# Order of slot 0's weight splits, its gates' gathers and the first weight conversions in a fused attention and two-MLP kernel

## The chip, the cores and the metric

One core of one Trainium2 chip runs the whole program. The metric is the time of one execution on the device, in microseconds (us). A core has TensorE (PE: matmuls; PEld: its weight loads), VectorE (DVE), ScalarE (ACT), GpSimd (POOL) and SyncE (SP). Each engine takes its own instructions strictly in order and waits on semaphores for the others. DMAs are issued by SyncE and, where the rows are picked by an index list, by GpSimd.

## The reference, cut to what matters

```python
x = attention(q, k, v)        # windowed and block-summary attention, 2 x 768 tokens, 8 heads of 64
idx = argmax(normalised(x) @ normalised(expert_emb).T / tau)     # one of 8 experts for a token
out[mask_e] = gate[mask_e] * (relu(x[mask_e] @ w1[e]) @ w2[e])    # 512 -> 1024 -> 512, for each expert e
h = out @ w_in                                                    # 512 -> 2048
g = (a0 + a1*h + a2*h*h + a3*h**3) / (1 + |b0|*|h| + |b1|*h*h + 1e-6)
return g @ w_out                                                  # 2048 -> 512
```

The precision wanted is that of float32, so a product is computed as three: high half by high half, low half by high half, high half by low half. A "split" makes the halves of one block of 128 x 1024 weights: ScalarE copies the block rounded into `whi` (`shi`), and `slo` subtracts that from the block to give `wlo`.

## The kernel before, in words

**Stages.** Attention and the router run first, up to about 102 us. The tokens are then sorted by expert into slots of 128 rows (17 in this run), and the slots are worked off one by one up to about 316 us. The dense second MLP follows, up to the end.

**A slot.** `gather(s)` (GpSimd, indirect DMA) fetches the slot's 128 rows from `xs` in DRAM into one of three buffers `xg`. `xtr(s)` transposes them on TensorE; ScalarE makes the high half (`xhi`, for slot 1 the upper part of `hhi`), VectorE the low half. `gemm1(s)` multiplies by w1 in 24 matmuls of 512 columns. For the first three slots it runs eight with the high half of x, then eight with its low half (the low pass), then eight with `wlo`. `relu(s)` is on ScalarE. `htr(s)` transposes the hidden rows in two halves (ScalarE high, VectorE low). `gemm2(s)` multiplies by w2 in 24 matmuls, and `gemm2e(s)` scales by the gate in `gts` on ScalarE. The program issues `gemm1(s)` before `gemm2(s - 1)`, so TensorE works on two slots in turn.

**Weights.** `wload(s, part)` has SyncE load four blocks of 512 KB of w1 (part 0) or w2 (part 1). From slot 2 on, a load is made only where a flag in the table `rg` says that the expert changes. `wsplit(s, part)` does the splits of four blocks under the same flag, for which ScalarE and VectorE each load the flag of `rg` into a register (lines 896 and 904, `values_load`) and branch. Slots 0 and 1 always have the weights of experts 0 and 1, but `wsplit(1, 0)` reads its flag all the same. Slot 0's splits are not conditional: `l0` to `l3` in the list below are the low splits of its w1 blocks, `slo(0, 4 + k)` those of its w2 blocks.

**The table.** `table()` is a chain of 16 small steps on VectorE, each `tb` in the list being one. The last (lines 758 to 773, called the tail here) writes all of `rg`: each slot's expert, the row of its results, and the flags. The list of row indices for the gathers does not need the tail.

**The written-out order.** `DRAIN` (lines 65 to 68) is the order by hand of the work between attention and the slots: `g0`, `g1` are gather(0) and gather(1), `x0` is xtr(0), `z0`, `z1`, `rc`, `rg` are the gates' softmax (`rg` here is `router_g`, lines 527 to 531, not the table), `F5` gives the indices of slots 1 and on, `k2b` is two matmuls that only keep TensorE busy. `SE` names the engine of `l0` to `l3`, D for VectorE and P for GpSimd. After it the program continues with lines 1161 to 1249.

**Gates.** A slot's gate is column 512 of its row in `xs`, stored by `gw` (SyncE) once `router_g` is done. Slots 0 and 1 are gathered before that, so `regather` fetches their rows once more, and `gate0` copies the column into `gts`, on GpSimd. From slot 2 on, VectorE copies it in `xtr` (line 685).

**Conversions.** The second MLP's weights are stored as 64-bit words. While the slots run, jobs of 128 x 512 words (two a slot) turn them into float32: `conv_load` (SyncE), `conv_a` (ScalarE), `conv_c` (a clamp, GpSimd, line 926), `conv_b` in three steps (VectorE, lines 931 to 937), `conv_s` (store).

Of the kernel before, what the change touches and what calls it, by code (L numbers as in the profile page):

```python
# [58 lines left out]
STOP = False  # L59
MICRO = True  # L60
TRACE = []
SE = "DDDD"
NX, NM = 22, 26
TS, OS = (), (0, 2)
DRAIN = ("E4 T2 h3 E4 S E4 w8 w9 O3 M O2 T1 Z8 O1 d3 X m8 E3 E3 m8 E3 f9 E2 E2 E2 T0 f10 Z9 E1 u3 p3 p3 p3 u3 u3 R0 "
# [3 lines left out]
NEG = 1.0e30  # L69
RS = 1536  # L70
NA = E * RS // P
# [10 lines left out]
def tile_kernel(ctx, tc, I, out):  # L82
    nc = tc.nc
# [457 lines left out]
    def wload(s, part, ks=range(4)):  # L541
        r = rw[s % 2, part]
        src = I["w1"] if part == 0 else I["w2"]
        if s > 1:
            ev = nc.sync.value_load(rg[0:1, 1, s:s + 1], min_val=0, max_val=E - 1)
            fl = nc.sync.value_load(rg[0:1, 3, s:s + 1], min_val=0, max_val=1)
        for k in ks:
            if s < 2:
                nc.sync.dma_start(out=r[:, k], in_=src[s, :, k])
            else:  # L550
                nc.sync.dma_start(out=r[:, k],
                                  in_=src[bass.ds(ev, 1), :, k].rearrange("o p f -> (o p) f"), cond=fl > 0)
# [95 lines left out]
    def gather(s):  # L648
        xg[s] = gx[s % 3]
        nc.gpsimd.indirect_dma_start(out=xg[s], out_offset=None, in_=xs,  # L650
                                     in_offset=bass.IndirectOffsetOnAxis(ap=idx[:, s:s + 1], axis=0))
# [38 lines left out]
    def slo(s, i, eng):  # L690
        eng.tensor_tensor(out=wlo[:, i], in0=rw[s % 2, i // 4][:, i % 4], in1=whi[:, i].bitcast(F32), op=ALU.subtract)  # L691
# [232 lines left out]
    def conv_c(j, eng):  # L924
        z = cvt[j][1].bitcast(F32)
        eng.tensor_scalar(out=z, in0=z, scalar1=CLO, scalar2=CHI, op0=ALU.max, op1=ALU.min)  # L926
# [23 lines left out]
    hsb = {}  # L950

    def gemm1(s, between=None):
        hi, lo = xTm.pop(s)
        if s == 1:
            ph = [ps_g.tile([P, 4, P], F32, name="hg").rearrange("p a b -> p (a b)") for n in range(2)]
        else:
            ph = [ps_h.tile([P, 512], F32, name=f"ph{n}") for n in range(2)]
        for rl in (False, True):
            ls = (hi,) if rl else (hi, lo)
            knl = [(k, n, l) for k in range(4) for n in range(2) for l in ls]  # L960
            if s < 3:
                knl.sort(key=lambda x: x[2] is lo)
            for k, n, l in knl:
                if between and l is lo and (k, n) == (2, 0):
                    between()
                w = (wlo if rl else whi)[:, k, 512 * n:512 * n + 512]
                nc.tensor.matmul(out=ph[n], lhsT=l[:, k], rhs=w, start=(k == 0 and not rl and l is hi),  # L967
                                 stop=(k == 3 and rl))
        hsb[s] = (hb, ph)
# [4 lines left out]
            nc.scalar.activation(out=h[:, 4 * n:4 * n + 4], in_=ph[n].rearrange("p (a b) -> p a b", a=4),  # L974
                                 func=AF.Relu)

    def htr(s):
        h, _ = hsb.pop(s)
        hi, lo = hhl
        for n in range(2):  # L980
            pt = ps_ht.tile([P, 4, P], F32, name=f"pht{n}")
            for k in range(4):
                nc.tensor.transpose(out=pt[:, k], in_=h[:, 4 * n + k], identity=ident)
            c = slice(4 * n, 4 * n + 4)
            nc.scalar.activation(out=hi[:, c], in_=pt, func=AF.Copy)  # L985
            nc.vector.tensor_tensor(out=lo[:, c], in0=pt, in1=hi[:, c].bitcast(F32), op=ALU.subtract)  # L986
        hTm[s] = (hi, lo)
# [159 lines left out]
    def regather(s):  # L1147
        nc.gpsimd.indirect_dma_start(out=xg[s], out_offset=None, in_=xs,
                                     in_offset=bass.IndirectOffsetOnAxis(ap=idx[:, s:s + 1], axis=0))

    def gate0(s):
        regather(s)
        nc.gpsimd.tensor_copy(out=gts[:, s:s + 1], in_=xg.pop(s)[:, DM:DM + 1])

    NSL = MAXS - 2
# [6 lines left out]
        conv_load(j)  # L1162
    gw()
    gather(2)
    gate0(0)
    gather(3)
    gemm1(0, lambda: xtr(1))
    gate0(1)
    wload(2, 0)
    wload(1, 1)  # L1170
    for j in job_at[2]:
        conv_load(j)
    wsplit(1, 0)
    relu(0)
    for k in range(2, 4):
        shi(0, 4 + k)
    for k in range(2):
        slo(0, 4 + k, nc.vector)
    for s in range(1, NSL + 1):
        mine = job_at.get(s, ())  # L1180
        if s == NX // 2 + 1:
            cx_.close()
            xb = ctx.enter_context(tc.tile_pool(name="xb", bufs=1, reuse_waits="tile"))
            x2.append((xb.tile([P, 4, TT], F32R, name="x2h0"), xb.tile([P, 4, TT], F32R, name="x2l0")))
        if 1 < s < NSL - 2:
            gather(s + 2)
        if s > 1:
            ysave(s - 2)
        if s >= NSL - 2:
            fsplit(s - (NSL - 2), 0)  # L1190
        if s >= NSL - 3:
            fload(s - (NSL - 3), 0)
        if s < NSL:
            gemm1(s)
            if STOP and s == 1:
                cx_.close()
                moe.close()
                rawr.close()
                return
            if s == 1:  # L1200
                htr(0)
                for k in range(2, 4):
                    slo(0, 4 + k, nc.vector)
                wload(2, 1)
            if s + 2 < NSL:
                wload(s + 2, 0)
            if s >= NSL - 6:
                x2load(s - (NSL - 6))
            for j in job_at.get(s - 1, ()):
                conv_s(j)  # L1210
            for j in job_at.get(s + 1, ()):
                if s > 1:
                    conv_load(j)
            if 1 < s < NSL - 1:
                wload(s + 1, 1)
            if s + 1 < NSL:
                wsplit(s + 1, 0, "h")
            relu(s)
            if s + 1 < NSL:
                if s != 1:  # L1220
                    xtr(s + 1)
                wsplit(s + 1, 0, "l")
            for j in mine:
                conv_a(j)
            for j in mine:
                conv_c(j, nc.gpsimd)
        if s > 0:
            gemm2(s - 1)
            if s == 1:
                xtr(2)  # L1230
            if s == NSL - 1:
                wsplit(s, 1, "h")
                htr(s)
            if s == NSL:
                elem_a(0)
                fsplit(3, 0, nc.gpsimd)
                elem_b(0)
            gemm2e(s - 1)
            if s == NSL - 1:
                wsplit(s, 1, "l")  # L1240
                fg1(0)
            if 0 <= s - (NSL - 5) < 4:
                x2prep(s - (NSL - 5))()
        if s < NSL - 1:
            htr(s)
            wsplit(s, 1)
        for j in mine:
            for k in range(3):
                conv_b(j, k)
    fload(0, 1)  # L1250
# [289 lines left out]
```

## Time and profile before

| what | value |
|---|---|
| three runs | 597.63, 600.44, 600.63 us; median 600.44 |
| the profiled execution | 601.18 us, of which the span is 599.4 |
| busy: PE, DVE, ACT, POOL | 572.9 (96%), 475.9 (79%), 418.1 (70%), 265.6 us (44%) |
| mean granted TensorE clock | 0.987 of full speed |
| chain that ended last | it can be followed back to 327.19 us; almost all of it is PE: matmuls of line 1335 20% of the span, 946 to 948 5%, 5% and 4% |

The busy share is a mean over stages. The chain of waits, followed back from the last instruction, runs through TensorE's matmuls alone until the last 27 us, and it says nothing of the slots, since TensorE has no pause there from which it could step to another engine. For these one reads the stretches (how long TensorE is idle in each), then its waits, and then each engine's time line, where the bracket behind a row gives the idle time before an instruction and what ended it. A row's start minus the start of the row before it on the same engine is what an instruction costs its engine; its duration is a little longer, as neighbours overlap.

### The profile page before, as it was taken

How to read it: one execution, taken by the hardware profiler on the slowest of the kernel's cores; microseconds unless marked ns; L12 is line 12 of the kernel's file. 1: busy time of each engine (PE TensorE's matmuls, PEld its weight loads, DVE VectorE, ACT ScalarE, POOL GpSimd, SP SyncE). 2: the span in 40 equal slices, each digit the busy share in tenths (PEclk: the TensorE clock that was granted, in tenths of full speed). 3: DMA queues.
4: the chain of work that ended last, by engine and by line, in shares of the span. 5: the costliest groups of instructions: out<-in, count | busy, mean ns of one | idle time of the engine just before them, and what ended most of it. 6: DMA issues, size and time to landing. Idle time of an engine off the chain costs nothing. (4 is left out here: it accounts for less than half of the span.)

```text
span 599.4 us, 10320 instructions
## 1 busy us (share of the span) xinstructions
PE 572.9 (96%) x3149; PEld 467.7 (78%) x3149; DVE 475.9 (79%) x1032; ACT 418.1 (70%) x722; POOL 265.6 (44%) x281
## 2 busy tenths in 40 slices
PE   4879998999999999999999999999999999999995
PEld 3768985787888888888887888888888888888884
DVE  6999988969755797588767888988988777777885
ACT  6969845673625755467766998777778887767673
POOL 6476161157443461634132564523535664432334
PEclk9889997999999999999999999999999999999999
DMA  9988934577678997798983434020244300100101
GB/s 299 324 252 283 341 117 122 173 252 249 239 234 296 346 322 232 249 323 305 374 261 93 132 96 125 27 79 1 61 133 140 89 1 1 52 19 0 54 17 71
DMA packets 38750, 101.66 MB, mean 170 GB/s; under 512 B 6105, under 2 KB 6233, under 8 KB 38690
## 3 DMA queue, kind: packets, MB, share of 16 engines
q1 hardware_dynamic: 36210, 92.81, 46.4%
q0 software_dynamic: 2480, 8.15, 4.3%
q8 instruction: 26, 0.43, 0.3%
q14 instruction: 34, 0.28, 0.1%
HBM read 119.51 MB, written 19.18 MB: 231 GB/s over the span
## 5 line engine op out<-in xcount | busy, mean ns | idle before, releaser
L926 POOL TENSOR_SCALAR el<-el 128x512 f32<-128x512 f32 x32 | 66.5, 2088 | 92.5 <-ACT el L921 92.5
L691 DVE TENSOR_TENSOR wlo<-rw,whi 128x1024 fp32r<-128x1024 f32 x64 | 77.1, 1262 | 1.3 <-ACT whi L688 0.9
L1135 POOL TENSOR_TENSOR wlo<-el,whi 128x512 fp32r<-128x512 f32 (+1 forms) x32 | 40.9, 1278 | 73.2 <-ACT whi L1133 35.6
L688 ACT ACTIVATE whi<-rw 128x1024 fp32r<-128x1024 f32 x64 | 62.7, 1051 | 6.0 <-DVEq L905 3.9
L998 PE MATMUL py<-whi,hhi 128*128 128x512 f32 x136 | 53.8, 404 | 0.2 <-ACT hhi L985 0.2
L998 PE MATMUL py<-whi,hlo 128*128 128x512 f32 x136 | 52.7, 396 | 0.0
L967 PE MATMUL ph<-whi,xlo 128*128 128x512 f32 x128 | 48.8, 398 | 1.3 <-DVE gts L685 1.3
L967 PE MATMUL ph<-whi,xhi 128*128 128x512 f32 x128 | 49.8, 407 | 0.3 <-ACT xhi L681 0.3
L986 DVE TENSOR_TENSOR hlo<-pht,hhi 128x512 fp32r<-128x512 f32 x34 | 21.8, 681 | 28.9 <-ACT y L1005 16.2
L1119 ACT ACTIVATE el<-el 128x512 f32<-128x512 f32 (+1 forms) x50 | 30.8, 615 | 14.3 <-DVE el L1113 14.3
L946 PE MATMUL hg<-x2h,whi 128*128 128x512 f32 (+1 forms) x100 | 39.0, 390 | 0.0
L1335 PE MATMUL acc<-whi 128*128 128x512 f32 x128 | 38.8, 393 | 0.0
L947 PE MATMUL hg<-x2h,wlo 128*128 128x512 f32 (+1 forms) x100 | 38.7, 387 | 0.0
L948 PE MATMUL hg<-x2l,whi 128*128 128x512 f32 (+1 forms) x100 | 38.6, 386 | 0.0
L1335 PE MATMUL acc<-whi,wlo 128*128 128x512 f32 x128 | 38.5, 391 | 0.0
L1135 POOL TENSOR_TENSOR xlo<-el,xhi 128x512 fp32r<-128x512 f32 (+1 forms) x17 | 20.9, 1230 | 39.5 <-issue 21.0
L1335 PE MATMUL acc<-wlo,whi 128*128 128x512 f32 x128 | 38.4, 390 | 0.0
L1111 ACT ACTIVATE el<-hg,ab 128x512 f32<-128x512 f32 (+1 forms) x33 | 22.2, 674 | 23.0 <-PE hg L948 23.0
L1005 ACT ACTIVATE y<-py,gts 128x512 f32<-128x512 f32 x17 | 11.7, 686 | 36.9 <-PE py L998 36.8
L1120 ACT ACTIVATE el<-el,ab 128x512 f32<-128x512 f32 (+1 forms) x50 | 35.4, 708 | 1.6
L1113 DVE SCALAR_TENSOR_TENSOR el<-el,ab,hg 128x512 f32<-128x512 f32 (+1 forms) x33 | 24.1, 730 | 14.9 <-ACT el L1112 14.6
L1125 DVE SCALAR_TENSOR_TENSOR el<-el,ab,hg 128x512 f32<-128x512 f32 (+1 forms) x33 | 24.1, 729 | 14.6 <-ACT hg L1121 13.9
(600 smaller groups left out, 1654.5 us busy)
## 6 DMA issues: line engine op xcount, KB each, us to landing
rw<-w SPq DMA_DIRECT2D x136, 512.0 KB
cx<-wio SPq DMA_DIRECT2D x22, 512.0 KB
wf<-el SPq DMA_DIRECT2D x32, 256.0 KB
vw<-vp SPq DMA_DIRECT2D x16, 292.5 KB
ys<-y SPq DMA_DIRECT2D x17, 257.0 KB
xg<-wf SPq DMA_DIRECT2D x13, 256.0 KB
xs<-xall SPq DMA_DIRECT2D x12, 257.0 KB
x<-ys SPq DMA_DIRECT2D x12, 257.0 KB
```

The costliest lines, as they stand in the source:

```text
L688: nc.scalar.activation(out=whi[:, i], in_=rw[s % 2, i // 4][:, i % 4], func=AF.Copy)
L691: eng.tensor_tensor(out=wlo[:, i], in0=rw[s % 2, i // 4][:, i % 4], in1=whi[:, i].bitcast(F32), op=ALU.subtract)
L926: eng.tensor_scalar(out=z, in0=z, scalar1=CLO, scalar2=CHI, op0=ALU.max, op1=ALU.min)
L946: nc.tensor.matmul(out=o, lhsT=lh, rhs=rh, start=start, stop=False)
L947: nc.tensor.matmul(out=o, lhsT=ll, rhs=rh, start=False, stop=False)
L948: nc.tensor.matmul(out=o, lhsT=lh, rhs=rl, start=False, stop=stop)
L967: nc.tensor.matmul(out=ph[n], lhsT=l[:, k], rhs=w, start=(k == 0 and not rl and l is hi), stop=(k == 3 and rl))
L998: nc.tensor.matmul(out=py, lhsT=l[:, f], rhs=w, start=(f == 0 and not rl and l is hi), stop=(f == 7 and rl))
L1119: nc.scalar.activation(out=a, in_=a, func=AF.Abs)
L1120: nc.scalar.activation(out=r, in_=a, func=AF.Ln, bias=ab[:, 7:8])
L1135: eng.tensor_tensor(out=lo, in0=g, in1=hi.bitcast(F32), op=ALU.subtract)
L1335: nc.tensor.matmul(out=acc[q], lhsT=l[:, q * P - o:(q + 1) * P - o], rhs=r, start=start, stop=stop)
```

## The change

It has six parts:

- In `DRAIN` the low split `l0` goes ahead of `x0`, `l1` ahead of `z0`, `l2` ahead of `rg` (`router_g`), and the last `tb`, the table's tail, goes from ahead of `x0` to the end of the list.
- `l3` goes to GpSimd (`SE`), and so do the low splits of slot 0's w2 blocks 2 and 3 (blocks 6 and 7 of eight), which stood behind `htr(0)` on VectorE and now stand with the first two.
- `htr(0)` is cut in two: its first half is issued inside `gemm1(1)`, before the fifth matmul of the low pass, and its second half behind that product, with both `conv_a` between them on ScalarE.
- The first conversion's clamp goes to VectorE, and its `conv_b` goes from behind slot 1's w2 splits to ahead of `gemm2(0)`'s part of the program.
- On GpSimd `regather(0)` stays where it was, but `gate0(0)`, gather(3) and `regather(1)` go from around `gemm1(0)` to behind the first clamp, and `gate0(1)` behind `gemm2e(0)`.
- On SyncE `wload(1, 1)` goes ahead of `wload(2, 0)`.

```diff
@@ -59,13 +59,13 @@
 STOP = False
 MICRO = True
 TRACE = []
-SE = "DDDD"
+SE = "DDDP"
 NX, NM = 22, 26
 TS, OS = (), (0, 2)
 DRAIN = ("E4 T2 h3 E4 S E4 w8 w9 O3 M O2 T1 Z8 O1 d3 X m8 E3 E3 m8 E3 f9 E2 E2 E2 T0 f10 Z9 E1 u3 p3 p3 p3 u3 u3 R0 "
          "E1 m9 E1 p3 O0 m9 Z10 R1 E0 E0 h4 d4 E0 w10 w11 u4 m10 f11 p4 Z11 p4 m10 q10 q9 p4 C p4 q11 n0 n1 u4 m11 u4 n2 n2 "
          "i0 m11 h5 d5 n2 p5 PC k2a tb p5 n2 tb p5 n2 p5 F1 tb F2 g0 i2 tb n2 tb F3 k4b i1 tb tb tb tb tb i3 tb K0 k3a tb tb "
-         "K1 k1a tb K2 k1b tb j0 j1 F4 F5 g1 tb x0 k2b z0 z1 rc l0 rg l1 l2 l3 ")
+         "K1 k1a tb K2 k1b tb j0 j1 F4 F5 g1 l0 x0 k2b l1 z0 z1 rc l2 rg l3 tb ")
 NEG = 1.0e30
 RS = 1536
 NA = E * RS // P
@@ -974,10 +974,10 @@
             nc.scalar.activation(out=h[:, 4 * n:4 * n + 4], in_=ph[n].rearrange("p (a b) -> p a b", a=4),
                                  func=AF.Relu)
 
-    def htr(s):
-        h, _ = hsb.pop(s)
+    def htr(s, ns=(0, 1)):
+        h, _ = hsb[s]
         hi, lo = hhl
-        for n in range(2):
+        for n in ns:
             pt = ps_ht.tile([P, 4, P], F32, name=f"pht{n}")
             for k in range(4):
                 nc.tensor.transpose(out=pt[:, k], in_=h[:, 4 * n + k], identity=ident)
@@ -1149,7 +1149,6 @@
                                      in_offset=bass.IndirectOffsetOnAxis(ap=idx[:, s:s + 1], axis=0))
 
     def gate0(s):
-        regather(s)
         nc.gpsimd.tensor_copy(out=gts[:, s:s + 1], in_=xg.pop(s)[:, DM:DM + 1])
 
     NSL = MAXS - 2
@@ -1162,20 +1161,18 @@
         conv_load(j)
     gw()
     gather(2)
-    gate0(0)
-    gather(3)
+    regather(0)
     gemm1(0, lambda: xtr(1))
-    gate0(1)
+    wload(1, 1)
     wload(2, 0)
-    wload(1, 1)
     for j in job_at[2]:
         conv_load(j)
     wsplit(1, 0)
     relu(0)
     for k in range(2, 4):
         shi(0, 4 + k)
-    for k in range(2):
-        slo(0, 4 + k, nc.vector)
+    for k in range(4):
+        slo(0, 4 + k, nc.vector if k < 2 else nc.gpsimd)
     for s in range(1, NSL + 1):
         mine = job_at.get(s, ())
         if s == NX // 2 + 1:
@@ -1191,16 +1188,16 @@
         if s >= NSL - 3:
             fload(s - (NSL - 3), 0)
         if s < NSL:
-            gemm1(s)
+            gemm1(s, (lambda: htr(0, (0,))) if s == 1 else None)
             if STOP and s == 1:
                 cx_.close()
                 moe.close()
                 rawr.close()
                 return
             if s == 1:
-                htr(0)
-                for k in range(2, 4):
-                    slo(0, 4 + k, nc.vector)
+                for j in mine:
+                    conv_a(j)
+                htr(0, (1,))
                 wload(2, 1)
             if s + 2 < NSL:
                 wload(s + 2, 0)
@@ -1220,10 +1217,16 @@
                 if s != 1:
                     xtr(s + 1)
                 wsplit(s + 1, 0, "l")
-            for j in mine:
+            for j in mine if s > 1 else ():
                 conv_a(j)
             for j in mine:
-                conv_c(j, nc.gpsimd)
+                conv_c(j, nc.vector if j == 0 else nc.gpsimd)
+            if s == 1:
+                for k in range(3):
+                    conv_b(0, k)
+                gate0(0)
+                gather(3)
+                regather(1)
         if s > 0:
             gemm2(s - 1)
             if s == 1:
@@ -1236,6 +1239,8 @@
                 fsplit(3, 0, nc.gpsimd)
                 elem_b(0)
             gemm2e(s - 1)
+            if s == 1:
+                gate0(1)
             if s == NSL - 1:
                 wsplit(s, 1, "l")
                 fg1(0)
@@ -1244,7 +1249,7 @@
         if s < NSL - 1:
             htr(s)
             wsplit(s, 1)
-        for j in mine:
+        for j in mine if s > 1 else mine[1:]:
             for k in range(3):
                 conv_b(j, k)
     fload(0, 1)
```

## Rows read from the trace of the kernel before

**Rows 1.** stretches; columns: stretch, us, busy us of each engine (instructions), granted clock, DMA share, GB/s.

```profile
37.20:40.60 3.40, 0.44 (x2) 0.20 (x2) 3.33 (x8) 0.76 (x2) 3.24 (x4) 1.00 0.83 207
40.60:44.00 3.40, 3.29 (x16) 2.96 (x18) 2.96 (x20) 1.24 (x4) 3.09 (x5) 0.50 0.32 120
91.80:98.60 6.80, 6.80 (x46) 4.10 (x46) 5.04 (x38) 2.93 (x9) 0.60 (x1) 0.50 0.55 159
144.80:573.00 428.20, 427.89 (x1952) 347.95 (x1951) 332.96 (x483) 301.89 (x475) 185.17 (x155) 1.00 0.46 155
```

**Rows 2.** waits of TensorE, 95 to 330 us; columns: us, times, longest.

```profile
PE ph L967 <- DVE wlo L691: 0.4, 1, 0.4
...
PE py L998 <- ACT hhi L985: 0.2, 1, 0.2
```

**Rows 3.** time line of TensorE; columns: start, us, instruction, count [idle before it].

```profile
110.34 2.13 PE L967 MATMUL hg<-whi,hhi 128*128 128x512 f32 x8
112.31 2.03 PE L967 MATMUL hg<-whi,hlo 128*128 128x512 f32 x8
...
138.68 0.51 PE L967 MATMUL ph<-whi,xlo 128*128 128x512 f32 x1 [1.32 <-DVE gts L685]
...
142.30 2.34 PE L967 MATMUL ph<-wlo,xhi 128*128 128x512 f32 x8
```

**Rows 4.** time line of VectorE, behind slot 1's splits.

```profile
133.26 0.83 DVE L931 TENSOR_SCALAR el<-el 128x512 int32<-128x512 int32 x1 [1.82 <-POOL el L926]
```

**Rows 5.** time line of VectorE, 101.7 to 111 us.

```profile
101.84 0.51 DVE L758 TENSOR_TENSOR pr<-ge,dv 128x342 f32<-128x342 f32 x1
...
103.36 0.68 DVE L682 TENSOR_TENSOR xlo<-pht,xhi 128x512 fp32r<-128x512 f32 x1
103.96 0.24 DVE L482 TENSOR_TENSOR zs<-zs,m 128x96 f32<-128x96 f32 x1
...
104.52 1.22 DVE L691 TENSOR_TENSOR wlo<-rw,whi 128x1024 fp32r<-128x1024 f32 x1
105.66 0.24 DVE L529 TENSOR_REDUCE rw__710<-zs 128x12 f32<-128x96 f32 x1
...
106.29 3.43 DVE L691 TENSOR_TENSOR wlo<-rw,whi 128x1024 fp32r<-128x1024 f32 x3
```

**Rows 6.** time line of ScalarE, 102.5 to 118.5 us.

```profile
106.82 0.60 ACT L681 ACTIVATE hhi<-px__1802 128x512 fp32r<-128x512 f32 x1 [1.94 <-PE px__1802 L679]
107.78 3.91 ACT L688 ACTIVATE whi<-rw 128x1024 fp32r<-128x1024 f32 x4 [0.36 <-DVE wlo L691]
```

**Rows 7.** line 904, 100 to 130 us; columns: ns min/median/max, first and last start.

```profile
L904 ACTq TENSOR_LOAD <-rg x2: 273/387/501, 106.8 to 124.6; - x2
```

**Rows 8.** groups of GpSimd, 316 to 590 us; columns: busy us, mean ns | idle before.

```profile
L1135 POOL TENSOR_TENSOR wlo<-el,whi 128x512 fp32r<-128x512 f32 x31 | 40.1, 1295 | 70.6 <-issue 34.8 <-ACT whi L1133 33.0 <-DMA xg<-xs,idx 1.0
```

**Rows 9.** time line of GpSimd in the attention stage.

```profile
36.55 2.06 POOL L196 TENSOR_TENSOR kw<-qk,one 128x1128 f32<-128x1128 f32 x1
```

**Rows 10.** time line of GpSimd, 98 to 147 us.

```profile
102.19 0.99 POOL L650 DMA_INDIRECT xg<-xs,idx  x1 [2.98 <-DVE idx L809]
...
129.34 1.01 POOL L1153 COPY gts<-xg 128x1 f32<-128x1 f32 x1 [5.92 <-DMA xg<-xs,idx]
130.33 4.79 POOL L926 TENSOR_SCALAR el<-el 128x512 f32<-128x512 f32 x2
```

**Rows 11.** time line of VectorE in the attention stage.

```profile
36.12 2.66 DVE L190 COPY el<-ks 128x288 f32<-128x288 f32 x1
```

**Rows 12.** lines 190 and 448, all of the run; columns as in rows 7.

```profile
L190 DVE COPY kw<-ks x6: 311/314/770, 4.8 to 53.4; 128x288 f32<-128x288 f32 x6
...
L448 DVE TENSOR_TENSOR oh<-cst,i x6: 145/176/583, 53.6 to 93.5; 128x16 bf16<-128x16 f32 x6
```

**Rows 13.** instructions and gathers on tile xg, 97 to 147 us.

```profile
L679 PE MATMUL px__2176<-cst,xg x4: 272/272/273, 130.1 to 130.4; 128*128 128x128 f32 x4
...
DMA to landing us min/median/max: 3.4/4.5/8.3
```

## The prediction

> **What bounds the kernel now.** I read the stretches first, then what TensorE waited for, then the time lines of the engines around slot 0. From 144.8 us to 573 us TensorE is busy for 427.89 of 428.20 us [rows 1]: whatever time it has at 144.8 us reaches the end unchanged, and no later stall is there to swallow a gain or a loss. The change touches only the stretch from 102 to 145 us, so the question is when TensorE gets to slot 2's second product, at 144.8 us in this trace. Before that its waits are few: 0.4 us for slot 0's low weights, 0.2 us for slot 0's hidden rows [rows 2], and the largest, 1.32 us for the low half of slot 3's rows [rows 3]. The cause of the last is readable: VectorE stood 1.82 us for GpSimd's clamp of the first conversion [rows 4], so xlo came late and TensorE resumed at 138.68 us. With the slower pace around these waits all this is some 3 us, 0.5% of the run, and that is about what a measurement can tell from no change: the change cannot win much more.
>
> **Part 1: slot 0's splits ahead of the table's tail.** The tail (the last `tb`) writes the table `rg`. VectorE now runs it from 101.84 us to xlo's start at 103.36, 1.52 us [rows 5]. Behind it stand xlo (0.60 us to the next start), z0 and z1 (0.56), a split (1.14), the gates' sums (0.63) and three more splits [rows 5]. In the new order VectorE does split 0, xlo, split 1, z0, z1, split 2, the sums, and only then the tail; split 3 goes to GpSimd. Split 0 fits in front of xlo, which needs ScalarE's high half first; I leave its start at 103.36. So 103.96 + 1.14 + 0.56 + 1.14 + 0.63 = 107.4 us for the tail's start and 109.0 for its end. The splits themselves come in time, which takes away TensorE's 0.4 us wait for them and the slower pace around it: the first product ends near 109.2 us instead of 110.3, where slot 1's begins now [rows 3].
>
> Who waits for the tail? `wsplit(1, 0)` is conditional: ScalarE loads a flag of `rg` into a register (line 904) before it may make slot 1's four high weight blocks. In this trace the flag is over 3 us old by then and costs only its load. The load is issued behind hhi at 106.82 and the first block starts at 107.78, 0.95 us later [rows 6]; the load itself takes 0.27 to 0.50 us [rows 7], so 0.72 to 0.95 us lie between flag and block, and I take 0.85, between the two. In the changed kernel ScalarE stands at that load until the table exists: 109.0 + 0.85 = 109.8 us instead of 107.78. Queued behind it on ScalarE are the four blocks, relu(0), slot 0's high blocks 6 and 7 and the high halves of the hidden rows, and TensorE waits for each of these. The one wait removed is replaced by a longer one.
>
> **Part 2: split 3 on GpSimd beside VectorE's split 1.** No row shows a 128x1024 subtraction on GpSimd. Twice the 128x512 one is 2.59 us [rows 8], and a product with 1128 columns took 2.06 [rows 9]; I take 2.4, nearer to the same operation. It starts when gather(1) has been issued, 102.19 + 0.99 = 103.2 us [rows 10], and ends about 105.6, before TensorE wants it. The price is on VectorE. A copy of 0.31 us [rows 12] took 2.66 when it met a GpSimd product from 36.55 to 38.61: it ended 0.17 us after that one [rows 9, 11]. That copy reads one SBUF tensor; an operation that reads two (L448) took 583 ns once against 145 to 176 [rows 12]. So split 1, which wants to start at 103.96, is held until shortly before GpSimd is done, 105.5 us: +1.6. The ends are nothing, if splits are not held, and the whole 2.4, if the order falls badly. With 1.6 the table is ready at 110.6 and ScalarE's first block starts at 111.4 us, 3.6 later than now. The Trainium skill (SBUF — State Buffer, section "SBUF: two separate sides") says that VectorE and GpSimd share a port pair under an exclusive lock held for a whole instruction, and names VectorE operations with two SBUF inputs among those that it stops. The rows agree as far as they go, and by that page a split that is not held, rival A below, would be ruled out.
>
> The consequence on TensorE: the four blocks take 3.91 us [rows 6], so the last is ready at 115.3; two matmuls later, at 115.8 us, the low pass of slot 1 begins. Now it begins at 112.31 [rows 3]. **+3.5 us.**
>
> **Part 3: slot 0's hidden rows transposed inside slot 1's product.** The eight transposes are the same; with four of them earlier, gemm2(0) need not wait for the first half. That saves the 0.2 us wait [rows 2] and about as much of the time that the transposes took ahead of it. **-0.4.** gemm2(0) starts 3.1 us late.
>
> **Part 4: blocks 6 and 7 on GpSimd.** Their high parts now come near 117 us; two splits of 2.4 us, alternating with VectorE's last one, end near 124.0. gemm2(0) wants them at about 125.6: hidden, with 1.6 us to spare. Without that cover each microsecond would be one of TensorE's.
>
> **Part 5: gathers and gates.** On GpSimd the gate of slot 0, gather(3) and slot 1's second gather now stand behind those two splits and a clamp. The two clamps took 4.79 us and a gate's copy 1.01 [rows 10]: 124.0 + 2.4 + 1.0 puts gather(3) at 127.4 us. xtr(3) begins at 130.1 now [rows 13] and would begin at 133.2 with the 3.1 us. From issue to landing gathers took 3.4 to 8.3 us, median 4.5 [rows 13]; beside the weight loads, as here, slot 1's second gather left GpSimd idle for 5.92 us after it was issued [rows 10]. So gather(3) lands between 130.8 and 135.7, a wait of 0 to 2.5 us. With the 5.92 and 1 us for the issue it would be 1.1; with the median it is none. I take **+0.7**, nearer to the row with the loads beside it. The gates themselves are wanted by y(0), which is late too.
>
> **Part 6: the first conversion.** Its clamp moves to VectorE, whose nearest row is a pass with two operators over the same 512 columns, 0.83 us [rows 4]. Four passes of at most that, from about 123 us on, end before xlo(2) is wanted, eight matmuls into slot 2's product (129 us): hidden. xlo(3) then waits for nothing on GpSimd: the 1.32 us wait goes, with the refill behind it 1.5; and the eight matmuls from 142.30, which took 2.34 us behind low splits that were late for the same reason, come to the 2.03 of those from 112.31 [rows 3], 0.3 less. **-1.8.** What is late next is xtr(3), above.
>
> **Part 7: SyncE.** The gates' store goes out when the sums are done, some 2.7 us later; slot 1's second half now goes ahead of slot 2's flagged load and needs no flag, so it starts earlier. It is wanted only after gemm2(0): no cost, and no gain, as nobody waits for it now.
>
> **Sum.** 3.5 - 0.4 + 0.7 - 1.8 = +2.0 us. The profiled execution took 601.18 us (span 599.4 and 1.8 around it), which gives 603.2. The median of the runs is 600.44, 0.74 lower: 602.4 us, 0.3% slower, within what can be told from no change.
>
> **Rivals.**
> *A, splits are not held by GpSimd's.* For it: none of the forms seen held is a split. The table is there at 109.0, the low pass 1.8 late, gemm2(0) 1.4, gather(3) in time: 1.4 - 1.8 = -0.4, 600.0 us. Against it: L448.
> *B, the table is not what ScalarE waits for* (an earlier write meets its flag's wait). Slot 1's low pass then starts 0 to 0.4 us earlier, and parts 3 and 6 give 2.2: -2.4, 598.0 us. For it: the load shows no wait now. Against it: the flags are written in the tail (line 773).
> *C, slower: the clock falls.* TensorE has nothing to do from 109.2 to about 112.5 us. From 37.20 to 40.60 it was busy for 0.44 us, and the stretch behind that ran at the lower level, 1.2 GHz, for 3.4 us; another low stretch lasted 6.8 [rows 1]. The price is decided at 115.8 us: up to there ScalarE sets TensorE's pace and half speed costs nothing. A fall from 112.5 us for 6.8 ends at 119.3 and costs half of 3.5 us: +1.7, 604.1 us, over 0.5% slower.
> *D, slower: GpSimd's chain is later still* (gather(3) lands after 8.3 us): +1.8, 604.2 us.
>
> **Chances.** Forecast 0.53 (601.2 to 604.0), A 0.18, B 0.07, C 0.12, D 0.10. Slower by over 0.5% (above 603.4): C, D and 0.08 of the forecast's own, 0.30. Faster by over 0.5% (below 597.4): the outer half of B, 0.04. Within: 0.66. The range takes in the forecast, A, C, D and half of B: 598.4 to 605.4 us.
>
> **What would show it.** Right: ScalarE's first block of slot 1 starts near 111.4 us, behind VectorE's line 773 and a register load; VectorE's second split of slot 0 lasts 2.5 us or more beside GpSimd's; VectorE waits for no clamp before slot 3; slot 2's second product begins near 146.8. Wrong: a first block at 107.8 (B), a split of 1.2 us (A), a granted clock under 1.0 after 109 us (C). If TensorE has stalls after 145 us that it does not have now, the whole reckoning fails.

## The result and the profile after

The changed kernel took 608.01 us (median of 6 runs, 604.68 to 608.88) against 600.11 us (597.1 to 602.53) for the kernel before. The medians lie 7.9 us apart, 1.3%; the ratio on record is 1.0104, 95% interval 1.0072 to 1.0136. Run again unedited, beside other runs of the kernel before (last experiment), the ratio came to 1.0060, 1.0030 to 1.0091. So it is slower, by 0.6 to 1.3%, 4 to 8 us. The forecast was +2.0 us, 602.4 us, in a range of 598.4 to 605.4.

The profiled execution took 608.6 us (span 606.7, mean granted clock 0.980 instead of 0.987). Three stretches of it, read from the trace:

- From slot 2's second product on, TensorE is still busy almost without a gap, as in [rows 1]; from there to the end it is 454.55 us, and 454.53 before. Nothing behind that point gains or loses.
- Slot 0's first transposes (xtr(0)) begin at 103.31 us instead of 101.93. The code ahead of them is the same.
- From xtr(0) to slot 2's second product ("the slot stage" below) it is 48.81 us instead of 42.90. These 5.9 us lie in the stretch that the change touches.

Stretches of the changed kernel; columns as in rows 1:

```profile
111.50:114.60 3.10, 0.30 (x2) 0.00 (x0) 1.69 (x8) 1.04 (x2) 0.00 (x0) 1.00 0.62 36
114.70:118.10 3.40, 3.40 (x8) 1.98 (x8) 3.40 (x4) 3.40 (x5) 2.58 (x2) 0.50 0.84 235
...
135.60:137.60 2.00, 0.14 (x1) 0.00 (x0) 1.97 (x4) 2.00 (x3) 0.00 (x0) 1.00 0.98 373
138.60:142.00 3.40, 3.40 (x10) 2.66 (x9) 0.43 (x2) 2.81 (x5) 1.16 (x2) 0.50 0.74 166
152.12:580.00 427.88, 427.57 (x1950) 347.72 (x1949) 329.50 (x478) 301.36 (x475) 184.39 (x155) 1.00 0.45 148
```

The first busy figure is TensorE's: 0.30 of 3.10 us, then 3.4 us at clock 0.50; 0.14 of 2.00 us, then 3.4 us at 0.50 again. Two long waits, each with a stretch at 1.2 GHz behind it. The time line of TensorE names them, and answers to [rows 3]:

```profile
109.37 2.44 PE L967 MATMUL ph<-wlo,xhi 128*128 128x512 f32 x8
114.67 3.83 PE L967 MATMUL hg<-whi,hhi 128*128 128x512 f32 x8 [2.86 <-ACT whi L688]
118.34 1.09 PE L967 MATMUL hg<-whi,hlo 128*128 128x512 f32 x4
119.27 0.60 PE L983 MATMUL pht<-cst,h 128*128 128x128 f32 x4
...
122.86 2.13 PE L998 MATMUL py<-whi,hhi 128*128 128x512 f32 x8
...
137.65 0.63 PE L679 MATMUL px__2176<-cst,xg 128*128 128x128 f32 x4 [1.90 <-DMA xg<-xs,idx]
```

The first wait, 2.86 us, is for ScalarE's high blocks of slot 1; the second, 1.90 us, for gather(3). VectorE shows why ScalarE was late (answers to [rows 5]):

```profile
103.38 1.23 DVE L691 TENSOR_TENSOR wlo<-rw,whi 128x1024 fp32r<-128x1024 f32 x1
104.64 0.69 DVE L682 TENSOR_TENSOR xlo<-pht,xhi 128x512 fp32r<-128x512 f32 x1
105.25 3.71 DVE L691 TENSOR_TENSOR wlo<-rw,whi 128x1024 fp32r<-128x1024 f32 x1
...
111.11 0.45 DVE L758 TENSOR_TENSOR pr<-ge,dv 128x342 f32<-128x342 f32 x1
...
112.49 0.17 DVE L773 TENSOR_TENSOR rg<-tb 128x18 int32<-128x18 f32 x1
```

Split 1 took 3.71 us where split 0 took 1.23; the table's last write, line 773, ended at 112.66. On GpSimd (answers to [rows 10]) stands what held it, and what came late behind:

```profile
103.52 1.92 POOL L650 DMA_INDIRECT xg<-xs,idx  x1 [2.98 <-DVE idx L809]
105.44 2.43 POOL L691 TENSOR_TENSOR wlo<-rw,whi 128x1024 fp32r<-128x1024 f32 x1
...
119.44 6.58 POOL L691 TENSOR_TENSOR wlo<-rw,whi 128x1024 fp32r<-128x1024 f32 x2 [0.48 <-ACT whi L688]
126.00 2.10 POOL L926 TENSOR_SCALAR el<-el 128x512 f32<-128x512 f32 x1
128.06 0.49 POOL L1152 COPY gts<-xg 128x1 f32<-128x1 f32 x1
128.83 1.07 POOL L650 DMA_INDIRECT xg<-xs,idx  x1 [0.28 <-POOL gts L1152]
```

The last row is gather(3), issued at 128.83 us instead of 121.18. ScalarE goes on as soon as the flag can be loaded. Line 904 (answers to [rows 7]; columns as there):

```profile
L904 ACTq TENSOR_LOAD <-rg x1: 469/469/469, 112.7 to 112.7; - x1
```

and the blocks behind it on the time line of ScalarE (answers to [rows 6]):

```profile
113.56 3.90 ACT L688 ACTIVATE whi<-rw 128x1024 fp32r<-128x1024 f32 x4 [3.27 <-DVE hlo L682]
```

From 112.66 to 113.56 it is 0.90 us. The view names hlo as what ScalarE waited for; the load at 112.7 us in its own queue says that it was the table. In the kernel before the same block starts at 107.78 us, ahead of hlo (109.63 us), so it does not need hlo.

### The profile page after: what moved, and what is told of

Read it like the earlier page. It is cut to its first block, busy times and chain, and to the rows that moved or that the text cites. A ratio compares the mean times of both kernels' runs of the same rounds, so it can differ in the third digit from the quotient of the medians.

```text
span 606.7 us, 10318 instructions
## 1 busy us (share of the span) xinstructions
PE 576.3 (95%) x3149; PEld 470.0 (77%) x3149; DVE 477.7 (79%) x1030; ACT 417.2 (69%) x722; POOL 271.7 (45%) x283
## 5 line engine op out<-in xcount | busy, mean ns | idle before, releaser
L926 POOL TENSOR_SCALAR el<-el 128x512 f32<-128x512 f32 x31 | 64.5, 2088 | 97.1 <-ACT el L921 90.9
L1111 ACT ACTIVATE el<-hg,ab 128x512 f32<-128x512 f32 (+1 forms) x33 | 22.2, 673 | 22.7 <-PE hg L948 22.7
L1113 DVE SCALAR_TENSOR_TENSOR el<-el,ab,hg 128x512 f32<-128x512 f32 (+1 forms) x33 | 24.1, 730 | 14.6 <-ACT el L1112 14.3
```

## The experiments

All figures but the ratio are from one profiled execution of each. Times after xtr(0) make executions comparable, since xtr(0) itself falls anywhere between 100.7 and 104.7 us in these traces. "Low pass" is the start of slot 1's low pass, "second" the start of slot 0's second product, "wait" that of xtr(3) for gather(3), "half clock" the stretches at 1.2 GHz from 105 to 145 us, "stage" the slot stage.

| kernel | low pass | second | wait | half clock, us | stage | ratio to before |
|---|---|---|---|---|---|---|
| before | 10.38 | 15.41 | 0 | none | 42.90 | 1 |
| changed | 15.03 | 19.55 | 1.90 | 114.7-118.1, 138.6-142.0 | 48.81 | 1.0104 (1.0072-1.0136) |
| changed, again | 15.26 | 20.63 | 0 | 114.3-121.1 | 46.23 | 1.0060 (1.0030-1.0091) |
| e1 tail ahead | 13.56 | 18.09 | 1.86 | 110.5-113.9, 137.8-141.2 | 47.28 | 1.0063 (1.0039-1.0087) |
| e2 split 3 on VectorE | 13.85 | 18.57 | 0 | 115.5-118.9 | 44.47 | 1.0060 (1.0029-1.0090) |
| e3 blocks 6, 7 on VectorE | 15.35 | 20.35 | 0 | 115.6-119.0 | 45.97 | 1.0063 (1.0033-1.0093) |
| e4 second wait filled | 15.33 | 20.74 | filled | 111.7-118.5 | 48.07 | 1.0108 (1.0063-1.0153) |
| e5 before, tail last | 15.14 | 21.31 | 0 | 111.8-118.6 | 46.90 | 1.0071 (1.0037-1.0104) |
| e7 before, parts 3 and 6 | 10.36 | 14.91 | 0 | none | 41.21 | 0.9963 (0.9938-0.9988) |
| e8 three undone | 10.49 | 15.02 | 0 | none | 41.59 | 1.0006 (0.9978-1.0034) |
| e9 before, split 3 on GpSimd | 12.05 | 17.06 | 0 | none | 44.56 | 1.0050 (1.0024-1.0077) |
| e10 both waits filled | 14.88 | 19.41 | filled | none | 46.76 | 1.0092 (1.0058-1.0127) |

**e1: the tail ahead again**

```diff
- F4 F5 g1 l0 x0 k2b l1 z0 z1 rc l2 rg l3 tb
+ F4 F5 g1 tb l0 x0 k2b l1 z0 z1 rc l2 rg l3
```

> The changed kernel with one thing undone: the table's last part stands ahead of slot 0's first split again. Theory (the late table starts a chain: ScalarE's blocks of slot 1, then GpSimd's splits of blocks 6 and 7, then gather(3), then the second clock fall): ScalarE's first block of slot 1 starts near 108 us instead of 113.56, the low pass of slot 1 near 113 instead of 118.34, gather(3) is issued some 4 us earlier so that xtr(3) waits for under 0.3 us, and no stretch at half clock falls between 114 and 145 us. 600 us (598.5 to 602), 6 to 9 us less than the changed kernel. Rival 1 (GpSimd's split beside VectorE's is the whole delay, the tail's place is not): the hold stays, so 605 or more. Rival 2 (gather(3) is late for its own reasons, the weight loads beside it, not for the table): the wait of 1.9 us at xtr(3) stays and with it the half clock near 140 us, about 603.5 us.

605.95 us: the theory's 600 us was missed by 6 us, and the time is that of rival 1, though the tail's place does cost by itself (e5). The hold didn't go, it moved. VectorE in e1:

```profile
104.56 2.74 DVE L763 TENSOR_TENSOR tb<-tb,cst 128x38 f32<-128x38 f32 x1
107.22 0.14 DVE L770 CAST rg<-cs 128x1 int32<-128x1 f32 x1
...
107.64 1.23 DVE L691 TENSOR_TENSOR wlo<-rw,whi 128x1024 fp32r<-128x1024 f32 x1
108.78 0.68 DVE L682 TENSOR_TENSOR xlo<-pht,xhi 128x512 fp32r<-128x512 f32 x1
```

and GpSimd's split in it:

```profile
104.82 2.42 POOL L691 TENSOR_TENSOR wlo<-rw,whi 128x1024 fp32r<-128x1024 f32 x1
```

An operation of 38 columns, 0.20 us elsewhere, stood until GpSimd's split ended at 107.24. Split 0, xlo and the router's values followed late, TensorE waited 2.35 us for xlo and ran at half clock behind that wait, gather(3) came 1.86 us late, and behind that the clock fell again, as in the changed kernel. The tail's place alone does not mend it.

**e2: split 3 on VectorE**

```diff
- SE = "DDDP"
+ SE = "DDDD"
```

> The changed kernel with slot 0's split 3 on VectorE instead of GpSimd. Theory (VectorE's split 1 lasted 3.71 us because GpSimd's split held it, and gather(1)'s issue was lengthened by VectorE's split): split 1 takes 1.2 us again, split 3 adds 1.14 behind the sums or ahead of the tail, so the table is ready 1.3 us earlier (line 773 ends near 111.2 instead of 112.66), the low pass of slot 1 starts 1.3 us earlier, and what hangs on it (gather(3), the half clock near 140 us) stays: 606.5 us (605 to 607.5). Rival 1 (split 1 was long for another reason): the table is 1.1 us later than in the changed kernel, 609 us or more. Rival 2 (the 1.3 us let gather(3) land in time and the half clock go): 603.5 us.

606.00 us, the theory's number, but by luck: the profile shows rival 2. gather(3) landed 0.1 us ahead of xtr(3)'s start, which it held up by 0.3 us at most, and the half clock near 140 us was absent. The stage is 4.3 us shorter than in the changed kernel; in this execution xtr(0) came 1.4 us later. Split 1 lasted 1.22 us:

```profile
106.62 1.22 DVE L691 TENSOR_TENSOR wlo<-rw,whi 128x1024 fp32r<-128x1024 f32 x1
```

The table ended 7.98 us after xtr(0) instead of 9.35: with one more split of 1.1 us ahead of it, that makes the hold 2.5 us.

**e3: blocks 6 and 7 on VectorE**

```diff
-    for k in range(4):
-        slo(0, 4 + k, nc.vector if k < 2 else nc.gpsimd)
+    for k in range(2):
+        slo(0, 4 + k, nc.vector)
...
                 htr(0, (1,))
+                for k in range(2, 4):
+                    slo(0, 4 + k, nc.vector)
```

> The changed kernel with the low splits of slot 0's blocks 6 and 7 on VectorE, behind the second half of the hidden rows, instead of on GpSimd. The late table stays. Theory (gather(3) waits in GpSimd's order behind those two splits of 6.6 us each pair, and its late landing is the 1.9 us wait ahead of xtr(3), behind which the clock falls): the low pass of slot 1 still starts near 118.3 us, gather(3) is issued 4 us or more earlier, xtr(3) waits for under 0.3 us, and the half clock from 138.6 to 142.0 us is gone: 604.5 us (603.5 to 606), 2.0 to 3.7 less than the changed kernel. VectorE's two splits of 1.2 us stand ahead of the clamp and xlo(2); if they make gemm2(0) or xlo(2) late, up to 1.5 us of it is lost. Rival 1 (gather(3)'s transfer, held up by the weight loads, lands near 137.5 us whenever it is issued): no change, 608 us. Rival 2 (the clock falls for what happened near 114 us, not for the wait near 137): the wait goes and the half clock stays, 606 us.

605.11 us. GpSimd issued gather(3) at 124.70 us, and it landed 4.3 us later; no wait, no second half clock, and the stage 2.8 us shorter. No wait of TensorE behind the two VectorE splits shows in the profile.

**e4: the second wait filled**

```diff
+                if s == 2:
+                    wt = ps_q.tile([P, DM], F32, name="py").rearrange("p (a b) -> p a b", b=P)
+                    for _ in range(8):
+                        nc.tensor.matmul(out=wt, lhsT=tri, rhs=one_b.unsqueeze(1).to_broadcast([P, 4, P]),
+                                         start=True, stop=True)
                 if s != 1:
                     xtr(s + 1)
```

> The changed kernel with eight more matmuls on constants, into a spare PSUM tile that nobody reads, put on TensorE ahead of xtr(3), where it waits for gather(3). Nothing else is moved. Theory (the wait itself costs some 2 us, and the half clock behind it, 138.6 to 142.0 us, 1.6 to 1.7 us more, because TensorE stood idle in the wait): the wait is filled with work that nobody needs, xtr(3) starts as late as before, but the granted clock stays at full speed behind it, and slot 2's second product begins 1.6 us earlier: 606.4 us (605.5 to 607.5). Rival (the clock falls whatever TensorE does in the wait, or the fall costs nothing): 608 us or, with the fillers partly in the way, up to 609.5.

608.56 us, with a wide interval: by the time alone nothing is gained. The last stretch of its profile runs at full speed (columns as in rows 1):

```profile
136.00:145.00 9.00, 9.00 (x46) 7.33 (x45) 6.85 (x10) 6.31 (x11) 6.65 (x5) 1.00 0.70 216
```

and the same stretch in the changed kernel does not:

```profile
136.00:145.00 9.00, 7.35 (x27) 5.99 (x28) 5.57 (x8) 5.62 (x9) 3.81 (x4) 0.81 0.78 253
```

From xtr(3) to slot 2's second product it is 12.88 us in e4 and 14.47 in the changed kernel: the 1.6 us that the half clock costs. That the fillers kept the clock up is not shown by it, for in this execution there was hardly a wait to fill. The first fall lasted 6.8 us instead of 3.4, so TensorE came to xtr(3) later. Its work ahead of the fillers ended at 134.9 us, and gather(3), issued at 126.94 us, landed 8.2 us later, at 135.1:

```profile
132.86 2.03 PE L967 MATMUL ph<-wlo,xhi 128*128 128x512 f32 x8
134.73 1.90 PE L1220 MATMUL py<-one_b,tri 128*128 128x512 bf16 x8
136.47 0.60 PE L679 MATMUL px__2185<-cst,xg 128*128 128x128 f32 x4
```

So the eight matmuls themselves held xtr(3) up, by some 1.2 us. The changed kernel run again (e11), with as long a first fall and no fillers, has no half clock there either, and its stage is 1.8 us shorter.

**e5: the kernel before with its tail last**

```diff
- F4 F5 g1 tb x0 k2b z0 z1 rc l0 rg l1 l2 l3
+ F4 F5 g1 x0 k2b z0 z1 rc l0 rg l1 l2 l3 tb
```

> The kernel before with one thing changed: the table's last part stands behind slot 0's last split, where the change puts it; all four splits stay on VectorE, gathers and the conversion stay as they were. From xtr(0) to slot 2's second product it is 42.9 us in the kernel before. Theory (ScalarE's blocks of slot 1 wait for the table, with no GpSimd split needed for it): the table ends 7.7 us after xtr(0) instead of 1.4, ScalarE's first block comes 0.9 us behind it, slot 1's low pass 2.6 us later than before; gather(3) is not moved and does not wait; so 45.5 us in the stage (44.9 to 46.1), and the run 2.0 to 3.2 us slower than the kernel before. Rival (the late table is harmless by itself, and only GpSimd's split, which holds VectorE, makes it late enough to matter): under 43.5 us in the stage and no change of the run.

605.98 us, 0.7% slower: the late table does it by itself, without GpSimd's split. The sizes were off, 46.90 us for the stage instead of 45.5. The table ended 9.2 us after xtr(0), not 7.7: xlo waits for ScalarE in any order, so that taking the tail out in front of it frees nothing, and VectorE stands 1.4 us idle. VectorE, and TensorE's wait behind the late table:

```profile
102.23 0.69 DVE L682 TENSOR_TENSOR xlo<-pht,xhi 128x512 fp32r<-128x512 f32 x1 [1.40 <-ACT xhi L681]
...
109.96 0.17 DVE L773 TENSOR_TENSOR rg<-tb 128x18 int32<-128x18 f32 x1
```

```profile
112.19 4.06 PE L967 MATMUL hg<-whi,hhi 128*128 128x512 f32 x8 [2.80 <-ACT whi L688]
```

The half clock then lasted 6.8 us. In return, with slot 0's second product 5.9 us late, the clamp of the first conversion was no longer late for slot 3: from that product to slot 2's it took 25.59 us instead of 27.49, with the conversion unchanged.

**e7: the kernel before with parts 3 and 6 alone**

```diff
-            gemm1(s)
+            gemm1(s, (lambda: htr(0, (0,))) if s == 1 else None)
...
-                htr(0)
+                htr(0, (1,))
...
-                conv_c(j, nc.gpsimd)
+                conv_c(j, nc.vector if j == 0 else nc.gpsimd)
+            if s == 1:
+                for k in range(3):
+                    conv_b(0, k)
...
-        for j in mine:
+        for j in mine if s > 1 else mine[1:]:
```

> The kernel before with only two parts of the change: half of slot 0's hidden rows transposed inside slot 1's product, and the first conversion's clamp on VectorE with its passes brought forward. Splits, table, gathers and gates stay as they were. Theory (the prediction's terms of -0.4 and -1.8 us were right): VectorE waits for no clamp ahead of slot 3's low half, TensorE's wait of 1.3 us there is gone, no half clock after 100 us; 40.7 us from xtr(0) to slot 2's second product instead of 42.9, and the run 1.5 to 2.5 us faster than the kernel before. Rival (these gains showed in the changed kernel only because everything else there was later): 42.5 us or more and no change of the run.

599.41 us (602.21 for the kernel before, beside it), ratio 0.9963 with an interval below 1: a version that beats both kernels, by about 2 us. The stage is 1.7 us shorter, where 2.2 was expected: 0.5 by the halves of the hidden rows, 1.2 by the conversion. VectorE still stood 1.83 us for GpSimd's clamp, now that of the second conversion, but slot 3's low half waited for ScalarE anyway. Of the 0.6 us missing from part 6's 1.8, 0.34 are a wait for the next late thing, slot 3's low split:

```profile
141.21 0.73 PE L967 MATMUL ph<-wlo,xhi 128*128 128x512 f32 x2 [0.34 <-DVE wlo L691]
```

**e8: tail ahead, and all low splits on VectorE**: the edits of e1, e2 and e3 together.

> The changed kernel with three things undone: the table's last part ahead of the first split, split 3 on VectorE, the low splits of blocks 6 and 7 on VectorE. The order of the gathers and gates, the halves of the hidden rows and the first conversion stay as the change has them. Theory (these three hold all of the loss): xlo and the router's sums come 1.1 us later than in the kernel before, which ScalarE's blocks follow by 0.3 us at most; slot 1's low pass 10.4 to 11.2 us after xtr(0) instead of 15.0, gather(3) in time, no half clock after 100 us; 41.5 us (40.5 to 42.5) from xtr(0) to slot 2's second product, and the run 0.5 to 2.4 us faster than the kernel before. Rival (the new order of gathers and gates costs something by itself): xtr(3) waits, 43.5 us or more, and the run no faster than before.

The stage came out as the theory had it, 41.59 us. The run did not: 602.13 us, 1.0006. Its profile has xtr(0) at 103.02 us instead of 101.93, and all but one of its times lie between 598.57 and 605.30 us, a spread wider than the effect. So the profile shows that these three edits hold the whole loss in the slot stage, and that what is left of the change beside parts 3 and 6 adds 0.4 us to it (e7: 41.21); that the kernel with them undone is faster than before is not shown.

**e9: the kernel before with split 3 on GpSimd**: the edit of e2 the other way round.

> The kernel before with one thing changed: slot 0's split 3 on GpSimd; the table's last part stays ahead. Theory (GpSimd's split of 2.4 us holds whatever operation on two SBUF tensors VectorE comes to, small or large, until it is done; what it costs depends on what stands there): one operation of VectorE between 103.3 and 106 us, z0, z1 or the first split, lasts 1.5 us or more longer than it does now; what follows it is needed soon, but one split fewer is left on VectorE, so the last low split is ready within 0.6 us of where it is now; 42.9 to 43.9 us from xtr(0) to slot 2's second product, the run between no change and 1 us slower. Rival (only large splits are held, or a split is not): no operation there lasts longer, VectorE is 1.1 us ahead, TensorE's wait of 0.4 us for the last low split goes, 42.5 us.

604.68 us, 0.5% slower, and a stage of 44.56 us, above the theory's 43.9. What stood there was the tail, as in e1. VectorE:

```profile
101.56 2.74 DVE L763 TENSOR_TENSOR tb<-tb,cst 128x38 f32<-128x38 f32 x1
```

GpSimd:

```profile
101.82 2.42 POOL L691 TENSOR_TENSOR wlo<-rw,whi 128x1024 fp32r<-128x1024 f32 x1
```

The gather's issue lasted 0.98 us here, the split began at 101.82, and xlo behind the tail began 2.4 us later after xtr(0) than in the kernel before; TensorE waited 1.13 us for it and twice 0.4 us for low splits. I had put the hold on z0 or a split, which have cover; the price is that of the operation that is hit.

**e10: both waits filled**: e4, and the same eight matmuls ahead of slot 1's first product.

> The changed kernel with eight matmuls on constants, into a spare PSUM tile that nobody reads, in each of TensorE's two long waits: ahead of slot 1's first product and ahead of xtr(3). Theory (the first fall of the clock, 114.69 to 118.10 us, follows the wait for the late table and costs only 0.4 us, because ScalarE's blocks set the pace there; the second costs 1.6): no half clock between 105 and 145 us, slot 1's low pass 14.6 us after xtr(0) instead of 15.0, 46.8 us (46.3 to 47.4) from xtr(0) to slot 2's second product instead of 48.81, and the run 1 to 3 us faster than the changed kernel. Rival (the first fall does not follow the wait; it comes anyway): half clock near 115 us as before, 47.2 us or more.

607.14 us, not faster than the changed kernel by its times. The profile has no half clock between 99 and 145 us, as expected; the low pass is at 14.88 (14.6 expected) and the stage 46.76, in the range:

```profile
112.00:122.00 10.00, 8.23 (x36) 5.54 (x35) 8.61 (x7) 8.61 (x12) 7.29 (x4) 1.00 0.92 301
```

The first fall therefore follows the wait, as far as one profile shows it. Of the second fall e10 says as little as e4: TensorE's work ended at 134.3 us and gather(3) landed at 135.4, and a wait of 1.3 us, ahead of slot 3's low half, had no half clock behind it in the kernel before [rows 3]. With the first wait filled, slot 0's second product comes 0.1 us earlier than in the changed kernel, whose fall lasted 3.4 us, and 1.2 to 1.3 us earlier than where it lasted 6.8 (e4, and the changed kernel again).

**e11: the changed kernel again**, unedited.

> The changed kernel again, nothing edited, profiled a second time beside the same runs of the kernel before as the others here. Theory (the loss lies in the slot stage and repeats; the 1.4 us by which the changed kernel's slot stage began later is chance): 48.8 us again (48.0 to 49.4) from xtr(0) to slot 2's second product, half clock in both waits again, xtr(0) anywhere between 100.5 and 105 us, the run 5 to 7 us slower than the kernel before. Rival (part of it was chance of that one execution, gather(3)'s late landing above all): under 47.5 us.

606.19 us, and the rival: stage 46.23 us, under 47.5. TensorE:

```profile
115.44 4.06 PE L967 MATMUL hg<-whi,hhi 128*128 128x512 f32 x8 [2.86 <-ACT whi L688]
119.29 1.91 PE L967 MATMUL hg<-whi,hlo 128*128 128x512 f32 x4
...
137.38 0.60 PE L679 MATMUL px__2176<-cst,xg 128*128 128x128 f32 x4
```

The first wait repeats to the hundredth. xtr(3) does not wait: gather(3) landed 7.4 us after its issue instead of 8.7, 0.3 us before it was wanted. The first fall lasted 6.8 us. So the late table is in both profiles of the changed kernel (9.35 and 9.40 us after xtr(0)); what follows it is partly chance. By the time after xtr(0), gather(3) landed 1.2 us earlier and TensorE came to xtr(3) 0.9 us later, and that decided over a wait of 1.9 us and another 1.6.

## Why the prediction was wrong

The chain was right, link by link: VectorE's second split held beside GpSimd's, ScalarE at the register load behind line 773, its four blocks late, no wait for a clamp ahead of slot 3, no stall behind 145 us. The sum was +2.0 us and should have been +3.3 to +5.9. Two terms failed: the table's, +3.5, which measured +4.65 and +4.88, and gather(3)'s, +0.7 with nothing for the clock behind it, which cost 1.9 and 1.6 us in one profile and nothing in the other. By stretches of the slot stage:

| from | to | forecast | changed | again |
|---|---|---|---|---|
| xtr(0) | low pass of slot 1 | +3.5 | +4.65 | +4.88 |
| low pass | slot 0's second product | -0.4 | -0.51 | +0.34 |
| that | slot 2's second product | +0.7 - 1.8 | +1.77 | -1.90 |
| sum | | +2.0 | +5.91 | +3.33 |

**Part 1 and 2, the table: mis-sized by 1.2 us.** Split 1 lasted 3.71 us, a hold of 2.5, where I took 1.6; the table ended 9.35 us after xtr(0), not 8.7. The 1.6 rested on GpSimd's split starting right behind a gather issue of 0.99 us [rows 10]. But the change puts VectorE's split 0 beside that issue, and it took 1.92 us: in all six profiles with that neighbour 1.91 to 1.92, and 0.98 in e1, e8 and e9, where something else stands there. So GpSimd began 0.9 us later and VectorE lost the whole of the split, the upper end that I had kept for the range. The link behind it was right: 0.90 us from table to block, 0.85 taken. The Trainium skill (SBUF — State Buffer, section "SBUF: two separate sides") has VectorE and GpSimd under an exclusive lock for a whole instruction, which goes to the one that starts first, and says that a DMA issued from GpSimd can't write its descriptors meanwhile. The last agrees with the 1.92 us, though the page names other VectorE operations for it; the prediction cites the section and does not hold this against the change. On the first come the traces differ, by the profile's start times: in e1 and e9 an operation of 0.20 us that began 0.26 us ahead of GpSimd's split ended just behind it, after 2.74. The other 0.4 us lie between the end of ScalarE's fourth block, 117.46 us, and the low pass, 118.34: 0.88 us where 0.5 was taken. In e10, with that stretch at full speed, it is 0.62, so 0.26 of them are the half clock on the high pass.

**Part 3: right**, 0.5 instead of 0.4, where the half clock is over in time; the changed kernel again lost 0.85 of it back to the clock.

**Part 4: hidden, as forecast.** The two splits ended 22.7 us after xtr(0), 0.6 later than forecast, and TensorE did not wait for them. What the prediction left out is VectorE: the pair took 6.58 us beside its six splits, and these took 9.12 instead of the 6.90 that they take where GpSimd doesn't split (e3). In e1, where only the last of VectorE's six was left, the pair took 4.92.

**Part 5 and rivals C and D: the step that failed.** I put gather(3)'s wait at 0.7 us, gave the clock's fall nothing in the sum, and held C and D for alternatives with 0.12 and 0.10. It is the landing that was mis-sized, not the queue ahead of it: gather(3) was issued 25.5 us after xtr(0) in both profiles, where the prediction has 127.4 - 101.93 = 25.5, and landed after 8.7 and 7.4 us, where a wait of 0.7 allowed 6.5. Issued 3.4 us earlier (e3) it was in time. They are neither rare nor alternatives. Both hang on the late table: a first fall came in each of the six profiles in which the table is late and nothing fills the wait, and in e1, where xlo is late instead; gather(3) was 1.9 us late in the changed kernel and in e1, and just in time in e2 and e11. Where it was late, in two profiles, half clock stands behind that wait too, and both add up: 1.2 us more wait than forecast and 1.6 of half clock. No run filled that wait, so that this second fall comes from it is argued from the first, not shown. The mark that the prediction set for C, a granted clock under 1.0 after 109 us, is there in all of these. C was priced well enough (1.7 us for a fall that lasts 6.8; 1.2 to 1.3 measured), but it was the rule. That D's wait would itself lower the clock was not in the prediction at all.

**Part 6: right in place.** No clamp is waited for and the last stretch of the table is 1.6 to 1.9 us shorter in e2, e3 and e11, where gather(3) is in time. But e5 shows that these terms don't add up as I added them: with the product late enough, the clamp's wait vanishes without any edit (1.9 us there), so beside the late table the part gains nothing of its own. Alone (e7) it is worth 1.2, and 0.9 in e8, where slot 0's product is early as well. (Part 7, SyncE's order, was not tested by itself.)

**Beyond the steps.** xtr(0) at 103.31 us is 1.4 us of the profiled execution's loss. In 12 traces with the same code ahead of it, it lay between 100.68 and 104.68 us, with falls of the clock at different places; I take it for chance, but that is not shown: the four kernels built on the one before lie at 100.68 to 101.93 us, the eight built on the changed one at 101.28 to 104.68, and e8, with a stage shorter by 1.3 us and no gain in time, would fit a later start too. By the ratios the stage is nearly all: 1.0104 of 600 us is +6.2, 1.0060 of 602 is +3.6, beside stages longer by 5.9 and 3.3 us in the two profiles. The medians (+7.9 and +4.2) leave room for more.

**What stays open.** Why gather(3) needs 4.3 us once and 8.7 another time. SyncE issues a run of four 512 KB weight loads 0.7 us apart at about that time. Gathers issued ahead of it landed after 4.2 to 6.2 us (before, e3, e7, e8, e9), those issued among its four after 7.3 to 8.7 (changed, again, e1, e2, e4, e10). e5 does not fit this: there it was issued at 114.85 us, 12.6 us ahead of that run, and landed after 8.2 us; eight other weight loads had been issued from 111.81 to 114.74 us. No run moved the loads by themselves, so that they are the cause is argued, not shown.

## What to carry to other kernels

A write that gates a register load is worth more than its place on its own engine says: follow it to the engine that stands at the load and to all that is queued behind. A big operation on GpSimd can be paid for by what VectorE has in hand at that moment, here a split (2.5 us) or an operation of 38 columns (2.5 us); look at what stands there, and what waits for it, rather than at the average. And where a change makes TensorE wait, put the half clock behind the wait into the sum, if the trace shows such stretches behind waits elsewhere [rows 1], and not among the rivals.

## What the runs showed of the hardware that was not expected

- A gather's issue on GpSimd went from 0.98 to 1.92 us with VectorE's 128x1024 split beside it.
- A VectorE operation of 38 columns, 0.20 us elsewhere, took 2.74 us though it began 0.26 us ahead of GpSimd's split (e1, e9).
- Two of GpSimd's 128x1024 splits, 2.40 to 2.44 us for a single one, took 6.6 us beside VectorE's six, and the six 9.1 us instead of 6.9.
- Behind TensorE's wait of 1.9 us for gather(3), with over 20 us of unbroken work ahead of it, stood 3.4 us at 1.2 GHz (changed kernel, e1); behind its wait of 1.3 us in the kernel before stood none. Behind the wait for ScalarE's blocks of slot 1, 2.06 to 2.87 us long, stood 3.4 or 6.8 us in six of six profiles, and none where eight matmuls filled part of it (e10).
